# Interleaving the leftover tokens, storing the last block over 128 partitions, and six-bank bursts, in a fused linear-attention and MLP kernel

## The chip, the cores and the metric

The kernel runs on one core of one Trainium2 chip. The metric is the device time of one execution in microseconds (us), the median of several executions; lower is better. Five engines work side by side on instruction streams of their own and meet only at semaphores: PE multiplies matrices, DVE and ACT work on vectors, POOL does the same[...], and SP issues transfers. PSUM has eight banks of 128 partitions by 512 numbers of 32 bits; in this program every matmul result lives in one bank or a half of one until DVE or ACT has read it.

## What is computed

The reference, cut to what matters:

```python
scale = 1 / sqrt(sqrt(64))
def phi(x):                                  # x: (8 batches, 8 heads, 576 tokens, 64)
    h = x @ omega.T - sum(x * x) / 2         # 128 features
    return exp(h - max(h)) / sqrt(128)
q_p, k_p = phi(q * scale), phi(k * scale)
kv  = einsum('bhsm,bhsd->bhmd', k_p, v);  z = k_p.sum(axis=2)
x   = (q_p @ kv) / (q_p @ z + 1e-6)          # attention, 4608 tokens x 512
h   = x @ w_in                               # 512 -> 2048
g   = h * clip(h + 3, 0, 6) / 6
out = g @ w_out                              # 2048 -> 512, float32
```

Each batch has 576 tokens. The kernel handles the first 512 of a batch as one block of the MLP (blocks 0 to 7). The last 64 tokens of each of the eight batches, the leftovers, are gathered in a buffer `xS` of 512 columns and are the ninth block, number 8.

## The kernel before

Every operation of the program is an object with its engine, the buffers that it reads and writes, and a function that emits it. They are numbered in the order in which the Python code makes them. A table `ORDER` lists, for each engine, those numbers in the order in which the engine is to run them. The waits follow from the buffers. So a change of the table moves work in time without changing what is computed.

**Attention scores in bursts.** From batch 3 on (`ROWS = 3`), the feature projections of keys and queries run as bursts. The contraction is only 64 long, so two matmuls run side by side in the upper and the lower half of the PE array. Between bursts PE works with the whole array.

```python
BURSTS = [[(0, 2)], [(2, 6)], [(6, 10)], [(10, 14)], [(14, 18)]]
...
def burst(n, ranges):
    parts = [(d0, d1, [Virt(ring, True) for _ in range(2 if d1 - d0 == 2 else 4)]) for d0, d1 in ranges]
    ...
    for part in parts:                       # e: one operation of PE
        for x in range(d1 - d0):
            for lh in range(2):
                E.matmul(...128 columns..., kT[64*lh:64*lh+64, d0+x, :], om[64*lh:64*lh+64, lh, :], ...)
        for lh in range(2):
            E.matmul(...256 or 512 columns..., om[64*lh:64*lh+64, lh, :], qT[64*lh:64*lh+64, d0:d1, :], ...)
```

A `Virt` is a PSUM bank held from the first write until the last read. A burst over two chunks holds two banks, one over four holds four. ACT reads each with `exp`.

**Leftover tokens.** After the attention of a batch its 64 leftover tokens lie in `xb`, one token to a partition. Batch 0 turns them on PE. The others turn them by a transposing transfer, straight into their 64 neighbouring columns of `xS`:

```python
op("SP", ..., lambda E: E.dma_start_transpose(
    xS[:, :, 64 * b:64 * b + 64], xb[pb][0:64, NJ * 512:XW]), ..., writes=[("xS", b)], group="dxS", ...)
```

**The MLP.** Block 0 and blocks 1 to 6 use 512-column matmuls for the first product (`mm1`); blocks 7 and 8 use a scheme with seven products in place of eight (`mm1_pair`), with sums of inputs and weights made beforehand (`x_sums`, `input_sums`). The second product uses that scheme from block 1 on (`products`), with sums of token activations made on POOL and, for the last block, also on DVE (`token_sums`, `last_sum`).

**The last block's stores.** A row of the result of block 8 is a leftover token of some batch. With batch after batch in `xS`, the 128 tokens of a quarter of the block come from two batches, so partitions 0 to 63 and 64 to 127 go to different places and each store is made twice, over 64 partitions:

```python
x = out.rearrange("(t a s) e -> a s t e", a=2, s=S)
parts = [(64 * a, 64, x[a, MAIN:S, 2 * i:2 * i + 2, c0:c1]) for a in range(2)]
```

The last product is cut in three (256, 128 and 128 columns), and each piece is added to what is there (`C12.8` on DVE) and stored, again twice:

```python
for n, (j, e0, e1) in enumerate(((0, 0, 256), (1, 0, 128), (1, 128, 256))):
    ... P8.6n on PE: 8 matmuls of e1 - e0 columns
    ... C12.8n on DVE: osb[:, j, 256+e0:256+e1] = psum + u3
    for x in range(2):
        ... E.dma_start(ends[x, MAIN:S, j, 256+e0:256+e1], osb[64*x:64*x+64, j, 256+e0:256+e1])
```

That makes twelve stores for block 8, issued from SP and ACT.

Of the kernel before, what the change touches and what calls it, by code (L numbers as in the profile page):

```python
# [20 lines left out]
        118, 13, 124, 139, 144, 156, 115, 150, 168, 147, 153, 133, 127, 121, 142, 162, 165, 183, 171, 159, 175, 177,  # L21
        136, 185, 212, 130, 173, 197, 214, 179, 219, 254, 199, 187, 181, 242, 227, 189, 204, 202, 257, 229, 244, 217,
        222, 403, 404, 232, 234, 415, 247, 416, 417, 409, 410, 249, 411, 405, 406, 412, 418, 207, 421, 424, 252, 237,
        260, 280, 427, 430, 433, 300, 436, 288, 284, 282, 439, 286, 442, 306, 303, 445, 290, 315, 324, 309, 448, 451,
        312, 292, 294, 454, 296, 318, 457, 298, 333, 321, 583, 584, 331, 573, 337, 574, 335, 575, 339, 585, 586, 587,
        327, 341, 588, 576, 353, 345, 589, 343, 577, 329, 355, 366, 578, 579, 593, 368, 379, 371, 594, 595, 358, 392,
        590, 384, 381, 394, 397, 580, 374, 596, 597, 598, 361, 387, 603, 400, 599, 600, 621, 627, 624, 639, 636, 604,
        630, 642, 645, 505, 651, 492, 660, 501, 654, 495, 657, 486, 605, 507, 511, 606, 503, 607, 474, 509, 666, 483,
        498, 477, 480, 672, 608, 669, 513, 489, 609, 792, 610, 675, 519, 782, 515, 517, 527, 783, 539, 798, 541, 544,
        532, 551, 785, 529, 786, 563, 793, 556, 565, 568, 553, 695, 795, 796, 702, 799, 801, 802, 723, 805, 806, 709,  # L30
        736, 809, 815, 716, 824, 812, 818, 830, 741, 827, 839, 833, 842, 748, 854, 848, 845, 750, 860, 738, 760, 857,
        772, 753, 863, 765, 970, 774, 777, 971, 762, 980, 973, 974, 981, 883, 986, 983, 984, 890, 987, 989, 990, 897,
        1003, 1000, 1012, 997, 993, 994, 1006, 911, 1015, 924, 1021, 1027, 929, 1018, 936, 1033, 1030, 904, 926, 1048,
        1042, 1036, 941, 938, 1045, 960, 1051, 1174, 1158, 1159, 965, 948, 962, 1168, 953, 950, 1161, 1071, 1169,
        1162, 1078, 1171, 1172, 1175, 1085, 1177, 1178, 1191, 1092, 1185, 1188, 1194, 1200, 1215, 1203, 1112, 1206,
        1209, 1218, 1181, 1182, 1124, 1117, 1224, 1221, 1230, 1236, 1114, 1099, 1239, 1233, 1126, 1136, 1346, 1347,
        1129, 1141, 1138, 1356, 1148, 1349, 1150, 1153, 1350, 1357, 1259, 1287, 1359, 1360, 1266, 1362, 1365, 1366,
        1273, 1363, 1379, 1376, 1373, 1382, 1388, 1300, 1394, 1369, 1302, 1312, 1391, 1305, 1314, 1397, 1370, 1317,
        1406, 1336, 1409, 1418, 1338, 1403, 1421, 1412, 1280, 1424, 1427, 1550, 1341, 1534, 1535, 1544, 1454, 1537,
        1545, 1447, 1324, 1538, 1326, 1329, 1547, 1548, 1461, 1551, 1553, 1468, 1557, 1554, 1488, 1475, 1490, 1558,  # L40
        1500, 1493, 1561, 1502, 1505, 1512, 1579, 1517, 1514, 1567, 1582, 1524, 1570, 1526, 1600, 1529, 1591, 1564,
        1615, 1609, 1594, 1576, 1606, 1585, 1612, 1660, 1673, 1597, 1663, 1629, 1665, 1676, 1702, 1630, 1668, 1678,
        1689, 1632, 1633, 1692, 1639, 1694, 1705, 1681, 1718, 1707, 1640, 1697, 1731, 1721, 1642, 1723, 1643, 1734,
        1710, 1747, 1736, 1648, 1649, 1760, 1726, 1750, 1739, 1807, 1645, 1763, 1752, 1646, 1765, 1820, 1755, 1810,
        1652, 1812, 1653, 1836, 1768, 1823, 1776, 1825, 1815, 1777, 1839, 1849, 1828, 1841, 1779, 1852, 1865, 1844,
        1854, 1780, 1878, 1868, 1786, 1857, 1870, 1881, 1787, 1894, 1883, 1792, 1907, 1873, 1886, 1897, 1789, 1899,
        1793, 1790, 1910, 1902, 1939, 1912, 1795, 1796, 1915, 1799, 1800, 1923, 1924, 1933, 1934, 1926, 1927, 1936,
        1937, 1940, 1943, 1944, 1960, 1952, 1956,
    ],
    "SP": [  # L50
        0, 21, 17, 32, 23, 22, 31, 19, 25, 26, 27, 24, 29, 28, 30, 269, 270, 271, 469, 473, 472, 471, 470, 592, 602,
        468, 688, 467, 582, 693, 402, 692, 691, 694, 612, 689, 547, 535, 690, 559, 571, 572, 880, 879, 881, 804, 876,
        756, 744, 808, 768, 780, 882, 877, 781, 878, 992, 1067, 996, 1069, 1068, 1070, 932, 1065, 944, 968, 956, 969,
        1066, 1064, 1255, 1184, 1257, 1256, 1258, 1180, 1120, 1252, 1253, 1144, 1132, 1156, 1157, 1254, 1440, 1443,
        1445, 1446, 1368, 1372, 1444, 1441, 1320, 1442, 1344, 1308, 1332, 1345, 1496, 1520, 1508, 1532, 1556, 1560,
        1533, 1651, 1655, 1798, 1802, 1950, 1948, 1949, 1947, 1962, 1959,
    ],
    "ACT": [
        18, 20, 138, 119, 140, 145, 141, 157, 148, 154, 169, 151, 134, 166, 143, 211, 163, 184, 135, 172, 160, 196,
        176, 178, 241, 174, 186, 213, 225, 226, 180, 243, 182, 203, 190, 218, 188, 233, 407, 413, 419, 422, 425, 281,  # L60
        238, 261, 431, 253, 434, 428, 301, 289, 285, 437, 440, 287, 307, 443, 304, 446, 310, 449, 316, 452, 313, 455,
        325, 319, 297, 299, 295, 352, 334, 322, 336, 340, 332, 458, 342, 328, 338, 354, 378, 377, 330, 367, 344, 380,
        346, 393, 375, 362, 388, 401, 622, 591, 628, 625, 640, 631, 581, 601, 637, 643, 652, 646, 493, 661, 506, 655,
        496, 658, 502, 508, 512, 487, 504, 475, 478, 481, 673, 484, 499, 490, 667, 510, 526, 514, 611, 676, 538, 670,
        516, 520, 528, 518, 540, 550, 784, 561, 562, 787, 564, 696, 698, 700, 708, 705, 707, 703, 731, 726, 729, 701,
        724, 735, 728, 715, 714, 710, 737, 712, 816, 717, 810, 719, 813, 721, 819, 746, 828, 759, 831, 825, 840, 843,
        834, 770, 846, 722, 849, 761, 771, 855, 773, 861, 864, 858, 972, 888, 886, 884, 891, 893, 889, 896, 895, 900,
        975, 1004, 1001, 902, 898, 903, 920, 923, 998, 1013, 1007, 914, 912, 916, 1016, 1022, 1019, 1028, 917, 1034,
        1031, 907, 905, 910, 909, 1043, 1037, 946, 1049, 1052, 947, 1046, 1160, 949, 1076, 1072, 1074, 1163, 1084,
        1083, 1081, 1079, 1077, 1086, 1090, 1088, 1091, 1093, 1192, 1095, 1111, 1186, 1098, 1189, 1201, 1204, 1195,  # L70
        1134, 1123, 1207, 1216, 1210, 1125, 1097, 1225, 1219, 1222, 1231, 1237, 1102, 1100, 1105, 1137, 1234, 1240,
# [331 lines left out]
def _emit(nc, es, q, k, v, omega, w_in, w_out, out):  # L403
# [38 lines left out]
    def sbt(name, shape, dt):  # L442
        return es.enter_context(nc.sbuf_tensor(name, list(shape), dt))
# [1049 lines left out]
```

The softmax here doesn't subtract the row's maximum and nothing guards it: scores larger than these inputs give would overflow.

## Time and profile before

| what | value |
|---|---|
| device time, three runs | 309.53 us median (307.55, 309.53, 787.75) |
| the profiled run | 308.06 us on the device, 306.2 us from first to last instruction |
| PE clock granted | 0.998 of full |
| busy: PE, DVE, ACT, POOL | 97%, 80%, 69%, 76% of the span |
| chain that ended last | 79% PE, 10% POOL, 4% transfers |
| transfers | 44.88 MB in 90147 packets, mean 147 GB/s |

In the profile, an "L" with a number is a line of the kernel's source: L766 and L769 are the two kinds of matmul of a burst, L1047 is the first product of blocks 1 to 6, L1126 that of blocks 7 and 8, L1305 the second product, L1371 the last product, L1379 the last addition, L1383 and L1400 stores, L594 and L621 loads, L1233 the sums. "PE" counts matmuls and "PEld" the loading of the fixed operand, which overlaps. The ends of matmuls are modelled, so a matmul of 512 columns shows 379 ns though the next begins earlier: intervals between starts are to be used, not the durations. "SPq" and "ACTq" are the issuing of transfers on those engines.

### The profile page before, as it was taken

How to read it: one execution, taken by the hardware profiler on the slowest of the kernel's cores; microseconds unless marked ns; L12 is line 12 of the kernel's file. 1: busy time of each engine (PE TensorE's matmuls, PEld its weight loads, DVE VectorE, ACT ScalarE, POOL GpSimd, SP SyncE). 2: the span in 40 equal slices, each digit the busy share in tenths (PEclk: the TensorE clock that was granted, in tenths of full speed). 3: DMA queues.
4: the chain of work that ended last, by engine and by line, in shares of the span. 5: the costliest groups of instructions: out<-in, count | busy, mean ns of one | idle time of the engine just before them, and what ended most of it. 6: DMA issues, size and time to landing. Idle time of an engine off the chain costs nothing.

```text
span 306.2 us, 7368 instructions
## 1 busy us (share of the span) xinstructions
PE 297.7 (97%) x2798; PEld 210.4 (69%) x2798; DVE 245.7 (80%) x539; ACT 212.8 (69%) x511; POOL 233.7 (76%) x247
## 2 busy tenths in 40 slices
PE   7999999999999999999999999999999999999993
PEld 5668866545785468646856586647764788888883
DVE  3978887779898885798596877896889898999953
ACT  4995997578959972889477758876875876675300
POOL 2775657089894989799989896988845999999950
PEclk9999999999999999999999999999999999999999
DMA  8999999999972999999949984998906000210125
GB/s 224 297 187 187 269 163 153 209 206 181 194 187 35 165 143 182 242 155 208 175 104 124 217 222 112 131 130 215 207 20 190 9 0 3 94 45 3 69 88 120
DMA packets 90147, 44.88 MB, mean 147 GB/s; under 512 B 57984, under 2 KB 87808, under 8 KB 90112
## 3 DMA queue, kind: packets, MB, share of 16 engines
q1 hardware_dynamic: 62368, 30.98, 43.5%
q0 software_dynamic: 26592, 12.46, 34.1%
q10 hardware_dynamic: 1152, 0.98, 1.2%
q8 instruction: 22, 0.36, 0.5%
q14 instruction: 13, 0.11, 0.2%
HBM read 36.73 MB, written 9.44 MB: 151 GB/s over the span
## 4 chain that ended last, share of the span: by engine, by line
PE 79%; POOL 10%; DMA 4%; DVE 2%; issue 1%; SPq 1%; ACT 1%; POOLq 0%
PE p L1305 28%; PE p L1047 25%; PE p L1126 5%; PE p L1217 4%; POOL gT L1233 3%; PE p L1192 3%; PE p L978 3%; DMA wi<-in_moe_w_in_dram 3%; POOL s L1233 3%; PE p L950 2%; PE p L766 2%; PE p L769 2%; DMA q<-in_q_dram 1%; SPq L621 1%; PE p L830 1%
## 5 line engine op out<-in xcount | busy, mean ns | idle before, releaser
L1047 PE MATMUL p<-xT,wi 128*128 128x512 f16 x384 | 90.3, 379 | 0.0
L1055 DVE SCALAR_TENSOR_TENSOR gT<-tsb,p 128x512 f16<-128x512 f16 x96 | 62.8, 679 | 12.4 <-ACT tsb L1053 11.6
L1053 ACT ACTIVATE tsb<-p 128x512 f16<-128x512 f32 x96 | 55.4, 600 | 16.5 <-PE p L1047 12.3
L1047 PEld LDWEIGHTS p<-xT,wi 128*128 128x128 f16 x384 | 35.4, 98 | 38.0 <-issue 1.1
L1305 PE MATMUL p<-wo,gT 128*128 128x256 f16 x368 | 45.8, 273 | 0.1
L1233 POOL TENSOR_TENSOR s<-gT 128x512 f16<-128x512 f16 x30 | 34.8, 1161 | 6.8 <-DVE gT L1055 4.8
L1233 POOL TENSOR_TENSOR gT<-gT,s 128x512 f16<-128x512 f16 x31 | 35.8, 1155 | 5.2 <-PE p L1305 3.0
L1233 POOL TENSOR_TENSOR s<-gT,s 128x512 f16<-128x512 f16 x31 | 35.8, 1156 | 4.9 <-DVE gT L1055 2.9
L1305 PEld LDWEIGHTS p<-wo,gT 128*128 128x128 f16 x368 | 35.0, 98 | 6.1 <-issue 0.8
L1233 POOL TENSOR_TENSOR gT<-gT 128x512 f16<-128x512 f16 x31 | 36.1, 1164 | 2.4
L934 POOL TENSOR_TENSOR vc<-v,cc 128x512 bf16<-128x512 f32 x24 | 25.4, 1057 | 12.3 <-DVE cc L928 7.4
L790 DVE TENSOR_REDUCE mx<-kp 128x4 f32<-128x512 bf16 (+1 forms) x50 | 29.9, 619 | 5.0 <-ACT kp L785 5.0
L794 ACT ACTIVATE qpT<-p 128x512 bf16<-128x512 f32 (+1 forms) x50 | 26.9, 564 | 8.6 <-PE p L769 8.6
L785 ACT ACTIVATE kp<-p 128x512 bf16<-128x512 f32 (+1 forms) x50 | 26.2, 559 | 9.3 <-PE p L769 8.6
L1305 PE MATMUL p<-t,gT 128*128 128x256 f16 x256 | 31.4, 273 | 0.0
L994 DVE TENSOR_TENSOR xb<-p,rec 128x256 f16<-128x256 f32 (+1 forms) x64 | 28.8, 471 | 0.6
L621 POOL DMA_DIRECT2D qb<-in_q_dram x28 | 19.5, 705 | 11.5 <-PE p L1047 9.6
L1305 PEld LDWEIGHTS p<-t,gT 128*128 128x128 f16 x256 | 24.3, 98 | 5.1 <-issue 1.2
L522 ACT COPY p<-p 128x256 f32<-128x256 f32 (+1 forms) x46 | 17.7, 398 | 13.2 <-PE p L1126 5.6
L1174 ACT ACTIVATE tsb<-p 128x512 f16<-128x512 f32 x32 | 18.8, 598 | 6.5 <-PE p L1126 3.9
L621 POOL DMA_DIRECT2D kb<-in_k_dram x21 | 16.5, 786 | 7.1 <-PE p L1047 7.1
L1176 DVE SCALAR_TENSOR_TENSOR gT<-tsb,p 128x512 f16<-128x512 f16 x32 | 21.0, 679 | 0.9 <-ACT tsb L1174 0.8
(132 smaller groups left out, 580.4 us busy)
## 6 DMA issues: line engine op xcount, KB each, us to landing
v<-in_v_dram SPq DMA_DIRECT2D x14, 512.0 KB, 4.9
out_dram<-osb SPq DMA_DIRECT2D x14, 512.0 KB, 3.3
kb<-in_k_dram POOLq DMA_DIRECT2D x14, 256.0 KB, 5.4
qb<-in_q_dram POOLq DMA_DIRECT2D x14, 256.0 KB, 5.6
wo<-in_moe_w_out_dram POOLq DMA_DIRECT2D x8, 256.0 KB, 8.2
wi<-in_moe_w_in_dram POOLq DMA_DIRECT2D x3, 512.0 KB, 7.4
q<-in_q_dram SPq DMA_DIRECT2D x4, 256.0 KB, 4.5
vl<-in_v_dram SPq DMA_DIRECT2D x8, 128.0 KB, 4.1
```

What stands on the lines that cost most here:

```text
L621: lambda E: E.dma_start(dst, src), prio + 0.001 * turn_of[0], reads=gate, writes=keys,
L785: op("ACT", actt(128 * (d1 - d0)), lambda E, lh=lh, ko=ko, part=part: E.activation(ko, out_of(part, 0, lh)[0].rearrange("p (x m) -> p x m" ...
L790: op("DVE", dvet(128 * (d1 - d0)), lambda E, ko=ko, mo=mo: E.reduce_max(mo, ko, axis=AX.X), p0 + 0.01, reads=[("kp", 0, d, lh) for d in ra ...
L794: op("ACT", actt(128 * (d1 - d0)), lambda E, lh=lh, part=part: E.activation(qd[:, part[0]:part[1], lh, :], out_of(part, 1, lh)[0].rearrang ...
L934: return E.tensor_tensor(vcm[:, :, 0:D], v32[:, m, :, :], cbc, ALU.mult)
L994: op("DVE", dvet(128 * n), lambda E: E.tensor_tensor(xv(i0, i1), psum()[:, :, :, 0:64], rbc, ALU.mult), t + 0.01, reads=[vn, ("rec", ru)], ...
L1047: ins = E.matmul(ring.t[vh.slot], wi[:, c, 128 * f:128 * f + 128], xv[:, c, :], start=(c == 0), stop=(c == NJ - 1))
L1053: op("ACT", actt(512), lambda E: E.activation(tsb[tu][:], ring.t[vh.slot], AF.Relu, bias=0.5, scale=1.0 / 6.0), t - 0.1, reads=[vh], write ...
L1055: op("DVE", dvet(512), lambda E: E.scalar_tensor_tensor(gT[gu][:, f, :], tsb[tu][:], 1.0, ring.t[vh.slot], ALU.min, ALU.mult), t - 0.1, re ...
L1176: op("DVE", dvet(512), lambda E, v=v, tu=tu, dst=dst: E.scalar_tensor_tensor(dst(), pieces(tsb[tu][:]), 1.0, pieces(v.ring.t[v.slot]), ALU ...
L1233: op(engines, {"POOL": 0.07 + n / 455.0, "DVE": 0.1 + n / 850.0}, lambda E: E.tensor_tensor(dst, x, y, ALU.subtract if minus else ALU.add) ...
L1305: ins = E.matmul(ring.t[v.slot][:, 256 * j:256 * j + 256], a[:, f, 128 * j:128 * j + 128], w[:, f, :], start=(first and f == 0 and j == 0) ...
```

## The change

It has four parts.

1. The leftovers are interleaved: column 256·(b // 4) + 4·s + b % 4 of `xS` holds leftover token s of batch b. A transposing transfer[...] writes a small buffer `xs0`, and a copy on ACT or POOL puts it into `xS`. Batch 0 writes the pattern from PSUM directly.
2. With that, the 128 tokens of a quarter of block 8 are 32 tokens of four batches, which one pattern in memory can address. Each store of the last block goes once over 128 partitions: nine in place of twelve.
3. The first two bursts of a batch (two and four banks) become one of six banks.
4. A new table `ORDER` for all engines.

The diff without the table:

```diff
-    BURSTS = [[(0, 2)], [(2, 6)], [(6, 10)], [(10, 14)], [(14, 18)]]
+    BURSTS = [[(0, 2), (2, 6)], [(6, 10)], [(10, 14)], [(14, 18)]]
...
+    xs0 = [sbt("xs0_%d" % u, [128, NJ, 64], F16) for u in range(2)]
...
-            op(EV_T, both(256), evac(lambda: xS[:, :, 64 * b:64 * b + 64],
+            op(EV_T, both(256), evac(lambda: woven(b),
...
             op("SP", 0.6, lambda E: E.dma_start_transpose(
-                xS[:, :, 64 * b:64 * b + 64], xb[pb][0:64, NJ * 512:XW]),
-               pos(12), ..., writes=[("xS", b)], group="dxS", inc=16, lat=1.0,
+                xs0[pb][:], xb[pb][0:64, NJ * 512:XW]),
+               pos(12), ..., writes=[("xs0", pb)], group="dxS%d" % pb, inc=16, lat=1.0,
                name="Sdma.%d" % b, issue=1.2, packet=24.0)
+            op(("ACT", "POOL"), {"ACT": 0.4, "POOL": 0.6}, evac(lambda: woven(b), lambda: xs0[pb][:]), pos(12) + 0.05,
+               reads=[("xs0", pb)], writes=[("xS", b)], name="Swv.%d" % b)
+
+    def woven(b):
+        c = 256 * (b // 4) + b % 4
+        return xS[:, :, c:c + 253:4]
...
+    def leftovers(r):
+        s0 = MAIN + 32 * (r % 2)
+        return out.rearrange("(i b s) e -> i s b e", b=4, s=S)[r // 2, s0:s0 + 32]
...
-            for x in range(2):
-                op(("SP", "ACT"), ..., E.dma_start(
-                    ends[x, MAIN:S, j, 256 + e0:256 + e1], osb[64 * x:64 * x + 64, j, 256 + e0:256 + e1]), ...)
+            op(("SP", "ACT"), ..., E.dma_start(
+                leftovers(j)[:, :, 256 + e0:256 + e1], osb[:, j, 256 + e0:256 + e1]), ...)
...
-            x = out.rearrange("(t a s) e -> a s t e", a=2, s=S)
-            parts = [(64 * a, 64, x[a, MAIN:S, 2 * i:2 * i + 2, c0:c1]) for a in range(2)]
+            parts = [(r, 1, leftovers(r)[:, :, c0:c1]) for r in (2 * i, 2 * i + 1)]
```

The part of the table that orders the end, with the numbers turned into the operations that they stand for (`outw` and `outl` are stores of block 8, `outl` those of the last product's pieces):

| engine | before | after |
|---|---|---|
| PE | P8.3 P8.4 P8.5 P8.62 P8.60 P8.61 | P8.3 P8.4 P8.62 P8.61 P8.5 P8.60 |
| DVE | C22.8 u4.8 C21.8 C12.82 C12.80 C12.81 | C22.8 u4.8 C12.81 C12.82 C21.8 C12.80 |
| SP | outw ×4, outl2, outl1 | outw ×2, outl1, outl2, outw, outl0 |
| ACT | outw ×2, outl0, outl2, outl0, outl1 | outw ×3 |

At the start, SP's first eight loads of batch 0 were keys (left), keys, queries (left), queries, queries, queries (left), keys, queries. They become keys (left), keys, queries, keys, queries, queries, queries, queries (left): the 256 KB pieces of queries come earlier, the 64 KB pieces of leftover queries later. The first loads of `w_in` on POOL wait for one of those 256 KB pieces; it was the eighth load on SP and is now the sixth. On the vector engines some operations change places: of the copies into `xS`, those of batches 1, 2 and 5 are on ACT and those of 3, 4, 6 and 7 on POOL; of the sums near the end, three go from DVE to POOL and two from POOL to DVE.

## The prediction

> **What bounds the kernel now.** I read the table of stretches first. Columns: the stretch in us, its length, then the busy time of PE, PE's operand loads, DVE, ACT and POOL with instruction counts in brackets, the granted clock, the share of the transfer engines, GB/s.
>
> ```profile
> 20.00:30.00 10.00, 9.48 (x109) 7.79 (x109) 8.26 (x25) 6.42 (x16) 4.62 (x7) 1.00 1.39 185
> 30.00:100.00 70.00, 69.93 (x639) 45.88 (x637) 57.93 (x123) 57.35 (x137) 47.00 (x55) 1.00 0.96 177
> 100.00:228.00 128.00, 127.76 (x1241) 84.14 (x1240) 100.28 (x227) 94.36 (x234) 110.83 (x115) 1.00 0.98 164
> 228.00:290.00 62.00, 61.72 (x529) 50.02 (x528) 58.05 (x111) 39.54 (x89) 53.59 (x46) 1.00 0.15 49
> 301.40:306.20 4.80, 0.00 (x0) 0.00 (x0) 0.30 (x2) 0.00 (x0) 0.00 (x0) 0.84 0.66 145
> ```
>
> From 30 to 290 us PE is idle for 0.07 + 0.24 + 0.28 = 0.6 us in 260. Because matmul ends are modelled, "busy" alone proves little, so I check the rate on the chain of waits:
>
> ```profile
> 158.14 5.29 PE p L1047 x24
> 288.01 11.61 PE p L1305 x104
> ```
>
> The first is 220 ns for each 512-column matmul, the second 112 ns for each of 256. At the 2.4 GHz that the Trainium skill gives ("TensorE: Matmul & The Clock Gate", the part on the measured gap, which states columns over 2.4 GHz plus about 2.5 ns) these would be 216 and 109. The trace agrees within 3%. PE really streams. Counting by the groups by shape: 472 matmuls of 512 columns x 0.220 = 104 us; 1363 of 256 x 0.1105 (between the 0.109 of an undisturbed run and the 0.112 above) = 151; 576 of 65 columns, which in the timeline follow each other by some 31 ns, = 18; some 120 of 128 x 0.056 = 7; 32 of 130 x 0.06 = 2; the bursts, below, 15. The sum is 297 us, against a last matmul that ends at 301.4. So in the middle there are waits of a few tenths, in the first 30 us of about 3 (PE idle 2.04 before 10 us, then 0.53 and 0.52), and after the last matmul 4.8 us in which PE has nothing. 63 of the 256-column matmuls (7 us) are fillers that keep PE busy while it waits for the first data. The change can gain at the two ends and at the bursts; it removes no matmul.
>
> **The Trainium skill** on the parts concerned. "SBUF — State Buffer", section "Door 1", says that partitions 0 to 63 reach only 8 of 16 ports, so a 64-partition transfer has half the rate; "DMA: Bandwidth & Descriptors", section on the anatomy of one transfer, puts a fixed cost of about 2 us on each. The list of transfer issues agrees with the second and shows why the first matters little here:
>
> ```profile
> out_dram<-osb SPq DMA_DIRECT2D x4, 128.0 KB, 2.5
> out_dram<-osb ACTq DMA_DIRECT2D x2, 32.0 KB, 2.5
> ```
>
> A fourfold size doesn't change the 2.5 us to landing. "TensorEngine Tiling (Array Packing)", "Gotcha 1: PSUM Pressure", says that row tiles write different banks: a burst therefore asks for its banks all at once.
>
> **Part 1, the stores at the end.** The timeline of the last 5 us (start, length, engine, line, operation, count):
>
> ```profile
> 300.99 0.74 DVE L1379 TENSOR_TENSOR osb<-p,u 128x256 f32<-128x256 f32 x2 [0.43 <-PE p L1371]
> 301.04 1.26 SPq L1400 DMA_DIRECT2D out_dram<-osb  x2
> 301.12 0.27 PE L1371 MATMUL p<-wo,gT 128*128 128x128 f16 x2
> 301.44 2.60 ACTq L1383 DMA_DIRECT2D out_dram<-osb  x4
> 302.35 1.24 SPq L1383 DMA_DIRECT2D out_dram<-osb  x2
> ```
>
> The last addition ends at 300.99 + 0.74 = 301.73. Nothing is computed after that, yet ACT issues four stores until 304.04 (2.60 / 4 = 0.65 us each). The last of these starts about 303.4, lands some 2.2 us later, and the program closes 0.5 us after. From the last addition to the end: 306.2 − 301.73 = 4.45 us, of which some 1.7 us is the queue of issues. Afterwards the last product's pieces need three issues in place of six, and by the new order the pieces of 128 columns and their stores are done before the last matmuls. After the last addition (`C12.80`) only one store remains, and one on the same queue a little ahead of it (`outw`, released by `C21.8` about 0.4 us earlier, 0.62 us to issue). So: 0.2 us wait for the queue + 2.5 us to landing + 0.5 us close = 3.2 us, 1.25 less. Against that, the last piece on PE is now 256 wide, so its addition takes 0.42 and not 0.29 us, and `C21.8` (0.69 us) runs just before it: PE's end to DVE's end grows from 0.34 to about 0.6 us. **Net −1.0 us**, all on the path.
>
> **Part 2, six-bank bursts.** A burst alone, and two bursts that already lie side by side in the kernel before:
>
> ```profile
> 150.03 1.04 PE L1305 MATMUL p<-wo,gT 128*128 128x256 f16 x8
> 150.99 0.40 PE L766 MATMUL p<-om,kT 64*128 64x128 bf16 x8
> 151.23 0.38 PE L769 MATMUL p<-qT,om 64*128 64x512 bf16 x2
> 151.54 0.94 PE L1305 MATMUL p<-wo,s 128*128 128x256 f16 x7
> ...
> 180.73 0.60 PE L1305 MATMUL p<-t,s 128*128 128x256 f16 x4
> 181.26 0.29 PE L766 MATMUL p<-om,kT 64*128 64x128 bf16 x4
> 182.12 0.61 PE L1305 MATMUL p<-wo,s 128*128 128x256 f16 x4
> ```
>
> Eight matmuls from 150.03 at 0.109 reach 150.90; the burst starts at 150.99: 0.09 lost on entry. It streams four pairs of 128 columns and one of 512, 1024 columns or 0.427 us, to 151.42; the next starts at 151.54: 0.12 lost on exit. So 0.21 us a burst. For the two together: 181.17 to 181.26 on entry, 0.640 us of columns to 181.90, next at 182.12: 0.31 us, where two alone lose 0.42. A merge saves 0.11 us. There are five, one of them side by side before already: 4 x 0.11 = **−0.4 us**. It is on PE's path, if ACT empties six banks in time: four `exp` of 256 and four of 512 columns, at 0.39 and 0.60 us about 3.5 us with their overlaps, in which PE must live on the two other banks. The new order puts each of these bursts beside pieces of the second product, which hold a bank for a long time, and I count no loss for it.
>
> **Part 3, the interleaving.** Seven more copies of 128x256. On ACT a copy of that size (`xT` in the groups) is 0.37 us: 3 x 0.37 = 1.1 us at 69% busy, hidden. On POOL the only conversion, 128x512, is 0.61 us; I take 0.45 for half of it with a stride, an estimate: 4 x 0.45 = 1.8 us. Two of them precede the sums of the last block, where POOL is the nearly full engine: 53.59 of 62 us from 228 to 290, and nothing but sums at one per 1.23 us from 243 on. The moves of sums between the engines add one more (three in, two out) for POOL: 1.23 us. Late sums reach PE: before the pieces that start at 249.71 and 288.01 the chain of waits runs through POOL for several us, yet PE waited only 0.31 and 0.30 us there (from the starts of its matmuls). The new order regroups just these sums (`P8.2` comes first, the last `S4` goes to DVE). I count **+0.4 us**.
>
> **Part 4, the start.** The chain of waits in the first 30 us runs through the loads:
>
> ```profile
> 5.47 4.40 DMA q<-in_q_dram
> 19.88 8.67 DMA wi<-in_moe_w_in_dram
> 28.69 1.91 PE p L1192 x16
> ```
>
> `w_in` waits for that q piece, landed at 9.87 us, the eighth load of SP; it becomes the sixth, and two pieces of 64 KB are no longer ahead of it. Loads land about 0.6 us apart there, so the gate opens about 1 us earlier. But POOL now does a cast (0.61) and a copy between the pieces of `w_in`, and the last piece is still behind two key loads with the transfer engines full (share over 1). Of the 1 us I count half: **−0.5 us**.
>
> **The sum**: −1.0 − 0.4 + 0.4 − 0.5 = −1.5 us on a span of 306.2, so 304.7. The profiled run took 308.06 on the device, 1.9 above its span: 306.6. The three runs scatter by 2 us without the disturbed one, so a median may lie a little higher; I say **306.8**.
>
> **Rivals.** (a) POOL becomes the bound of the last two blocks. For it: 1.23 + 0.9 us more work in a solid stretch, and PE waits there for POOL already. Against it: DVE takes other sums and the order was made for it. It would give 306.8 + 1.3 = 308. (b) A six-bank burst finds the banks taken and PE waits for ACT: five times, at most some 0.6 us each, +3 us, or 309.5; for it speaks that ACT's reads of bursts already make the groups `kp` and `qpT` wait on PE in clumps, against it that before, two bursts side by side passed with 0.31 us. (c) The start gains all that is idle there, 3 us in place of 0.5: 304.3. Against it, the transfers share is over 1 from 10 us on. (d) The end gains nothing because landing dominates: 307.8; against it, the issues visibly queue for 1.7 us.
>
> **Range and chances.** (a), (b) and (d) bound the upper side, (c) the lower: 304.6 to 309.3. Faster by over 2% would need 303.3, beyond (c); slower by over 2% needs 315.7, six us of new waits in a PE stream that has 0.6. So 0.05 faster, 0.92 within 2%, 0.03 slower.
>
> **What would show it.** Right: from the last addition to the end about 3.2 us in place of 4.45, one store issued after it; 20 entries into bursts in place of 24, each merged one losing about 0.3; `w_in`'s first issue near 9.1 us; PE idle from 30 to 290 us no more than 1 us. Wrong: PE waiting for POOL sums by more than 1 us after 228; gaps before bursts above 0.2 us, ended by ACT; the last `w_in` piece landing later than 28.5 us.

## The result, and the profile after

The changed kernel takes **303.57 us** (median of five, 303.2 to 304.12) against 308.15 us before: a ratio of 0.985, 95% interval 0.982 to 0.988. Measured once more in a later set of runs beside the kernel before, it took 303.74 us at a ratio of 0.980 (0.976 to 0.985). So it is 1.5 to 2% faster. The prediction of 306.8 us and its range (304.6 to 309.3) both lie above that. The span of the profiled run fell from 306.2 to 301.8 us, by 4.4; 1.5 was predicted.

The table of stretches after, with the columns explained in the prediction (stretch, length, busy time of PE, its operand loads, DVE, ACT and POOL, clock, transfers):

```profile
20.00:30.00 10.00, 10.00 (x123) 8.88 (x122) 9.45 (x27) 8.23 (x20) 4.54 (x8) 1.00 1.37 185
30.00:100.00 70.00, 69.65 (x634) 45.65 (x632) 57.50 (x125) 57.29 (x141) 48.54 (x58) 1.00 1.09 177
100.00:224.00 124.00, 123.89 (x1178) 81.70 (x1176) 98.81 (x222) 91.72 (x227) 106.26 (x111) 1.00 0.96 168
224.00:286.00 62.00, 62.00 (x574) 50.79 (x573) 58.17 (x118) 40.96 (x94) 57.07 (x52) 1.00 0.15 45
```

From 20 to 30 us PE is no longer idle at all (0.52 us before). In the 62 us from 224 us POOL is busier than before in the like stretch (57.07 against 53.59 us), and PE is idle for 0.00. The rate of matmuls hasn't changed; on the chain of waits after:

```profile
66.62 4.32 PE p L1054 x20
```

4.32 / 20 = 216 ns for a 512-column matmul. The end, in the timeline (start, length, engine, line, operation, count, and in brackets what ended the idle time):

```profile
297.51 1.04 PE L1381 MATMUL p<-wo,gT 128*128 128x256 f16 x8
297.71 0.69 DVE L1328 TENSOR_TENSOR osb<-p 128x512 f32<-128x512 f32 x1 [0.56 <-PE p L1312]
298.43 0.54 SPq L1408 DMA_DIRECT2D out_dram<-osb  x1
298.58 0.42 DVE L1389 TENSOR_TENSOR osb<-p,u 128x256 f32<-128x256 f32 x1 [0.18 <-PE p L1381]
299.04 0.58 SPq L1392 DMA_DIRECT2D out_dram<-osb  x1
```

The last addition ends at 299.01 (298.58 + 0.42, rounded), one store is issued after it, and the program ends at 301.77: 2.76 us later, where it was 4.45.

**Where the 4.4 us are.** Busy time can't say, because matmul ends are modelled. So I took the intervals between the starts of all 2800 matmuls and subtracted from each the streaming time (columns over 2.4 GHz plus 2.5 ns, as in the prediction; in rows of equal matmuls the starts are 216 ns apart for 512 columns and 109 for 256). What remains was sorted by kind: the time of fillers, gaps over 30 ns (waits), gaps at the entry and exit of bursts, and small gaps.

| part | before | after | difference | predicted |
|---|---|---|---|---|
| fillers and waits before 45 us | 12.44 | 11.33 | −1.11 | −0.5 |
| waits from 45 us on | 1.42 | 0.79 | −0.63 | +0.4 |
| entries and exits of bursts | 4.64 (24) | 3.88 (20) | −0.76 | −0.4 |
| start of the last matmul to the end | 4.99 | 3.49 | −1.50 | −1.0 |
| gaps under 30 ns, rest | | | −0.4 | 0 |
| sum | | | −4.4 | −1.5 |

Every term came out better than predicted, so no single step explains the miss. The experiments take the terms one at a time. Two limits hold for all of them: the runs scatter (the kernel after from 303.2 to 305.6 us, the kernel before in one set from 307.5 to 312.5), in part with the landing of the first loads, and each profile is one run. So differences below 1 us are read in the trace, at the place concerned, and a median is used where it is larger. The kernel before drifts from one set of runs to the next (medians 308.2 to 310.8 us); ratios compare with the kernel before in the same set, and their 95% intervals stand in brackets.

### The profile page after: what moved, and what is told of

It reads as the page before. It is cut to its first block, busy times and chain, and to the rows that moved or that the text cites. A ratio compares the mean times of both kernels' runs of the same rounds, so it can differ in the third digit from the quotient of the medians.

```text
span 301.8 us, 7410 instructions
## 1 busy us (share of the span) xinstructions
PE 295.8 (98%) x2800; PEld 211.4 (70%) x2800; DVE 246.8 (82%) x547; ACT 214.5 (71%) x516; POOL 237.0 (79%) x255
## 4 chain that ended last, share of the span: by engine, by line
PE 91%; ACT 5%; DVE 2%; issue 0%; ACTq 0%
PE p L1312 32%; PE p L1054 25%; PE p L1133 8%; PE p L1199 5%; PE p L1224 5%; PE p L985 3%; PE p L957 3%; PE p L767 2%; PE p L770 2%; PE p L811 1%; PE p L831 1%; PE p L576 1%; ACT vc L943 1%; DVE mx L822 1%; ACT tsb L1060 1%; PE p L535 1%
## 5 line engine op out<-in xcount | busy, mean ns | idle before, releaser
L1240 POOL TENSOR_TENSOR gT<-gT 128x512 f16<-128x512 f16 x32 | 37.0, 1155 | 3.2 <-DVE gT L1062 1.0
L1240 POOL TENSOR_TENSOR s<-gT 128x512 f16<-128x512 f16 x31 | 36.2, 1167 | 3.8 <-DVE gT L1062 1.7
L1240 POOL TENSOR_TENSOR gT<-gT,s 128x512 f16<-128x512 f16 x30 | 34.7, 1157 | 2.4
L795 ACT ACTIVATE qpT<-p 128x512 bf16<-128x512 f32 (+1 forms) x50 | 27.6, 572 | 7.7 <-PE p L770 7.1
L941 POOL TENSOR_TENSOR vc<-v,cc 128x512 bf16<-128x512 f32 x22 | 23.4, 1064 | 9.5 <-DMA v<-in_v_dram 3.3
L523 ACT COPY p<-p 128x256 f32<-128x256 f32 (+1 forms) x42 | 16.4, 403 | 14.9 <-PE p L1312 8.6
L943 ACT ACTIVATE vc<-v,cc 128x64 bf16<-128x64 f32 x80 | 20.3, 348 | 0.0
```

The lines of the kernel that those rows point to most:

```text
L795: op("ACT", actt(128 * (d1 - d0)), lambda E, lh=lh, part=part: E.activation(qd[:, part[0]:part[1], lh, :], out_of(part, 1, lh)[0].rearrang ...
L941: return E.tensor_tensor(vcm[:, :, 0:D], v32[:, m, :, :], cbc, ALU.mult)
L943: ins = E.activation(vcm[:, i, 0:D], v32[:, m, i, :], AF.Copy, scale=cc[pb][:, c0 + i:c0 + i + 1])
L1240: op(engines, {"POOL": 0.07 + n / 455.0, "DVE": 0.1 + n / 850.0}, lambda E: E.tensor_tensor(dst, x, y, ALU.subtract if minus else ALU.add) ...
```

## The experiments

### The end: nine stores, or their order

**oldend**: nine stores, old order of the last pieces.

```diff
 PE:  P8.3 P8.4
-     P8.62 P8.61 P8.5 P8.60
+     P8.5 P8.62 P8.60 P8.61
 DVE: C22.8 u4.8
-     C12.81 C12.82 C21.8 C12.80
+     C21.8 C12.82 C12.80 C12.81
 SP:  outw outw
-     outl1 outl2 outw outl0          ACT: outw outw outw
+     outw outl2 outl1                ACT: outw outw outw outl0
```

> The kernel after with its nine stores, but with the old order of the last pieces: on PE the 256-column product P8.5 ahead of the three last pieces P8.62, P8.60, P8.61, on DVE C21.8, C12.82, C12.80, C12.81. Theory B (the order gives the gain of the end): four stores are released within 1.4 us and queue on two engines, so last addition to end is about 3.3 us in place of 2.76, less 0.3 for the narrower last piece: 303.8 to 304.2 us. Rival A (the number of stores gives it): 303.3 to 303.7 us, equal to the kernel after or a little shorter because the last piece has 128 columns.

**twelve**: the new order, but no interleaving, no copies, twelve stores.

```diff
-    c = 256 * (b // 4) + b % 4;  xS[:, :, c:c + 253:4]
+    xS[:, :, 64 * b:64 * b + 64]
-    leftovers(j)[:, :, 256 + e0:256 + e1]        # one store, 128 partitions
+    for x in range(2): ends[x, MAIN:S, j, ...]   # two stores, 64 partitions each
```

> The kernel after without the interleaving: batch after batch in xS, no copies from xs0, and twelve stores of 64 partitions for the last block; merged bursts and the new order of the end are kept. Theory A (the smaller number of stores gives the end its gain): the second store of the last addition queues for 0.6 us on one of the two issuing engines, so last addition to end grows from 2.76 to 3.4 to 3.9 us and the time to 304.2 to 304.8 us. Rival B (the order gives it, stores overlap on two issuing engines): 2.8 to 3.0 us from last addition to end, 303.4 to 303.8 us, or less, since seven copies of some 0.77 us on ACT and POOL are gone.

**oldend12**: both edits together.

> The kernel after with both halves of the new end undone: batch after batch in xS without copies, twelve stores, and the old order of the last pieces and of their stores; merged bursts, start and middle as in the kernel after. From the start of the last matmul to the end of the span: 4.99 us before, 3.49 after, 3.91 with twelve stores in the new order, 3.07 with nine in the old order. If stores and order act together: 4.8 to 5.0 us, so 304.9 to 305.3 us. If something else in the new order of the whole shortened the end: 3.9 us or less, 304.0 us.

| | time, us | ratio to before | last matmul to end | waits of PE after 280 us |
|---|---|---|---|---|
| twelve stores, old order (oldend12) | 306.3 | 0.989 (0.985–0.992) | 4.89 | 0.43 |
| twelve stores, new order (twelve) | 305.0 | 0.986 (0.983–0.989) | 3.91 | 0.31 |
| nine stores, old order (oldend) | 304.65 | 0.985 (0.982–0.988) | 3.07 | 0.30 |
| nine stores, new order (after) | 303.57, 303.74 | 0.985, 0.980 | 3.49 | 0.00 |

In the timeline of oldend12 the queue of the kernel before is back, six issues behind the additions:

```profile
298.56 0.74 DVE L1384 TENSOR_TENSOR osb<-p,u 128x256 f32<-128x256 f32 x2 [0.43 <-PE p L1376]
299.01 2.59 ACTq L1388 DMA_DIRECT2D out_dram<-osb  x4
299.92 1.24 SPq L1388 DMA_DIRECT2D out_dram<-osb  x2
```

and with nine stores in the same old order the last three are issued as fast as they are released:

```profile
298.31 1.32 SPq L1397 DMA_DIRECT2D out_dram<-osb  x2
298.32 0.74 DVE L1394 TENSOR_TENSOR osb<-p,u 128x256 f32<-128x256 f32 x2 [0.43 <-PE p L1386]
298.78 0.55 ACTq L1397 DMA_DIRECT2D out_dram<-osb  x1
```

In the traces either edit shortens the end: the stores alone by 4.89 − 3.07 = 1.8 us, the order alone by 1.0 us. They remove the same queue, so together they don't add up to 2.8 but give 1.4. With nine stores the tail is even shorter in the old order (its last piece is 128 wide), but there PE waits 0.30 us ahead of P8.5 for DVE to free a bank, so the two orders come to 3.37 and 3.49 us. The profiled run of oldend (303.39 us) was the fastest of its six; why its median is 1 us above that of the kernel after is not settled.

**best1, best3**: one 128-column piece ahead of P8.5 to cover that wait, the short pieces last; best3 also swaps the engines that issue the last two stores.

```diff
-PE:  P8.62 P8.61 P8.5 P8.60      DVE: C12.81 C12.82 C21.8 C12.80
+PE:  P8.62 P8.5 P8.60 P8.61      DVE: C12.82 C21.8 C12.80 C12.81
-best1:  SP outl1, ACT outl0
+best3:  SP outl0, ACT outl1
```

> The kernel after with another order of the last pieces: on PE P8.62, P8.5, P8.60, P8.61, on DVE C12.82, C21.8, C12.80, C12.81, so that one 128-column piece covers the wait for DVE that the old order showed before P8.5 (0.30 us) and the last addition is a short one. If both hold: 3.07 us from the start of the last matmul to the end as with the old order, without its wait, so 0.4 us less than the kernel after, 303.2 us. If the wait comes back or the stores queue: 303.6 us.

> The kernel after with the last pieces in the order P8.62, P8.5, P8.60, P8.61, as tried once, but with the 256-column store on SP and the last 128-column store on ACT. In the first try ACT took 0.86 us to issue the 256-column store and that one landed last. If the issue alone was to blame: 3.1 to 3.3 us from the start of the last matmul to the end, 0.2 to 0.4 us less than the kernel after. If an issue from ACT is always late here: 3.4 us or more, no gain.

best1 took 303.97 us (ratio 0.981, 0.978–0.984), best3 303.59 (0.980, 0.975–0.984) beside 303.74 for the kernel after in the same set. The wait before P8.5 disappeared in both. In best1 ACT needed 0.86 us for the 256-column store, which landed last: 3.46 us from the last matmul to the end. In best3 it is 3.21 us, 0.3 less than after, as expected. That is a tenth of a per cent, and no time shows it. From here the landing (some 2 us after the last issue) and the close are what is left.

### The bursts: banks, or entering and leaving the half-array form

The merged burst at 151 us in the timeline of PE alone, after:

```profile
151.41 0.29 PE L767 MATMUL p<-om,kT 64*128 64x128 bf16 x4
151.54 0.27 PE L770 MATMUL p<-qT,om 64*128 64x256 bf16 x2
151.65 0.39 PE L767 MATMUL p<-om,kT 64*128 64x128 bf16 x8
151.87 0.38 PE L770 MATMUL p<-qT,om 64*128 64x512 bf16 x2
152.18 0.50 PE L1312 MATMUL p<-t,gT 128*128 128x256 f16 x3
```

From 151.41 to 152.18 are 0.77 us, of which 0.64 stream: 0.13 on exit; with 0.10 on entry, 0.22 for a burst of six banks. A burst of four loses 0.10 + 0.12, the same, and one of two in the kernel before 0.10 + 0.11. So it is a cost for each entry, whatever the size.

One of the five merged bursts loses 0.31 us, as the two side by side in the kernel before did, from which the prediction took its size. There the array's form is not all. In the kernel before, with DVE and the operand loads of PE:

```profile
181.37 0.69 DVE L1321 TENSOR_TENSOR u<-p 128x512 f32<-128x512 f32 x1 [0.58 <-PE p L1305]
...
182.12 0.55 PEld L1305 LDWEIGHTS p<-wo,s 128*128 128x128 f16 x6 [0.35 <-DVE u L1321]
```

The product that follows the burst starts when DVE has read a bank (181.37 + 0.69 = 182.06). At the merged burst of 117.57 us, after, its next product waits for the same operation of DVE. So about 0.09 of the 0.31 us is a wait for a bank.

**split**: the burst cut in two, one operation of PE between the parts. **adjacent**: cut in two, nothing between.

```diff
-    BURSTS = [[(0, 2), (2, 6)], [(6, 10)], [(10, 14)], [(14, 18)]]
+    BURSTS = [[(0, 2)], [(2, 6)], [(6, 10)], [(10, 14)], [(14, 18)]]
 PE, for each batch b from 3 on:
-    R b.0               <next operation>
+split:     R b.0  <next operation>  R b.1
+adjacent:  R b.0  R b.1  <next operation>
```

> The kernel after, but with the first burst of each of the five batches cut again into one of two banks and one of four, with one operation of PE in full-array form between them. Theory A (each entry into and exit from the half-array form costs about 0.21 us on PE): five more entries and exits, 0.8 to 1.0 us longer than the kernel after, so about 304.5 us against 303.6. Rival B (what the bursts save is only turned into waits elsewhere, or six banks at once cost waits): no longer than the kernel after, 303.3 to 303.8. In the profile, A expects 25 entries in place of 20 and waits of PE elsewhere unchanged.

> The kernel after with the merged burst cut again into one of two banks and one of four, but side by side, with nothing between them. The array stays in its half form from one to the other. Theory E (the cost is entering and leaving the half form): the same 20 entries, so no more than 0.1 us for each of the five, 304.0 us against 303.6 at most, and spans within 0.5 us. Rival W (the cost of the cut is that the second burst waits for its own four banks): waits of 0.3 to 0.7 us at three of the five, 1 us or more longer, as when one operation lay between.

split took **307.08 us** (0.995, 0.993–0.997), 3.4 above the kernel after; adjacent took **303.70** (0.980, 0.976–0.983), as much as the kernel after. In adjacent the pair of 154.19 us streams as one burst (timeline of PE alone):

```profile
154.19 0.28 PE L772 MATMUL p<-om,kT 64*128 64x128 bf16 x4
154.31 0.27 PE L775 MATMUL p<-qT,om 64*128 64x256 bf16 x2
154.42 0.39 PE L772 MATMUL p<-om,kT 64*128 64x128 bf16 x8
154.65 0.38 PE L775 MATMUL p<-qT,om 64*128 64x512 bf16 x2
154.96 0.50 PE L1317 MATMUL p<-t,gT 128*128 128x256 f16 x3
```

0.77 us again. So the merge as such gives nothing; what counts is that the array stays in its half form. "TensorEngine Tiling (Array Packing)" of the Trainium skill says in its section "Key Properties" that changing the tiling mode drains the engine. The traces agree and give the price: about 0.10 us in, 0.12 out.

In split the five further entries cost 5 x 0.22 = 1.1 us, and a second cost came that theory A did not have. It falls not on the second part but on the next burst after it. In batch 4 the parts start at 119.75 and 121.59 us, neither late, and the next burst is due at about 124.0. Its timeline, with ACT, DVE, PE and PE's operand loads:

```profile
123.95 1.19 ACT L791 ACTIVATE kp<-p 128x512 bf16<-128x512 f32 x3
124.09 0.69 DVE L1333 TENSOR_TENSOR osb<-p,u 128x512 f32<-128x512 f32 x1 [0.18 <-PE p L1317]
...
124.64 0.22 PEld L772 LDWEIGHTS p<-om,kT 64*128 64x128 bf16 x8 [0.86 <-ACT kp L791]
124.64 0.40 PE L772 MATMUL p<-om,kT 64*128 64x128 bf16 x8 [0.58 <-ACT kp L791]
```

It starts when ACT has read banks for `kp`. In three of the five batches the next burst was late by 0.2 to 0.65 us beyond the entry, each time with ACT ending the wait, and after one first part PE waited 0.53 us for DVE. Why these three, and how the operation between the parts brings it about, is not shown. In all, the bursts lose 2.7 us more than in the kernel after, and waits from 45 us on 0.5 us more (new ones at 206.78 and 209.46 us): 3.2 of the 3.4 us. The profiled run, 308.43 us, was the slowest of 16 and lost 1.6 us more at its start, where `w_in` landed late.

### The start

**loads_old**: only SP's first loads in the old order. **front_old2**: all engines' operations of the first batch in the old order. **front_new**: the kernel before with all engines' operations of the first batch in the new order.

```diff
 loads_old, SP:
-k-left k q k q q q q-left ...
+k-left k q-left q q q-left k q ...
 front_old2, front_new: the table's entries for the first batch, on all engines, from the other kernel
```

> The kernel after with the old order of SP's first loads alone; all other engines as in the kernel after. Theory G (the gate: w_in waits for the sixth load in place of the eighth): w_in's first issue goes from 9.49 us to about 10.2, its last piece lands 0.5 to 1.5 us later, PE waits for it, 304.3 to 305.5 us. Rival E (the order of the other engines did it): within 0.3 us of the kernel after.

> The kernel after with the order of the kernel before for the first batch's operations on all engines. Theory S (the new start gives 1.1 us, as fillers and waits in the first 45 us say: 12.44 us before, 11.33 after): fillers and waits near 12.4 us in the first 45 us and 304.5 to 305 us. Rival N (the start is worth nothing, another part gave its share): 303.4 to 304.0 us.

> The kernel before with the order of the kernel after for the operations of the first batch only: its loads, the loads and casts of w_in, the attention of batch 0 and its first product. Nothing else is changed. Theory S (the new order of the start gives about 1 us: w_in's last piece lands at 26.95 in place of 28.55 us and the waits between 20 and 30 us, 1.28 us, disappear): 306.9 to 307.4 us against 308.15. Rival N (fillers and other waits take its place): 307.9 to 308.3 us.

loads_old took 305.45 us (0.986, 0.981–0.991), 1.7 to 1.9 above the kernel after. Fillers and waits in the first 45 us of its trace are 12.58 us against 11.33, so to undo SP's order alone in the kernel after costs 1.25 us. But not through `w_in`: its first issue moved to 10.48 us and its last piece landed at 28.25, and PE did not wait for it. The time was gone earlier:

```profile
12.20 0.61 POOL L529 CAST qb<-q 128x512 bf16<-128x512 f32 x1 [0.77 <-DMA q<-in_q_dram]
...
12.86 0.67 PEld L540 LDWEIGHTS p<-ident,qb 128*128 128x128 bf16 x12 [0.39 <-POOL qb L529]
12.86 0.84 PE L540 MATMUL p<-ident,qb 128*128 128x128 bf16 x12
```

A query piece lands late, POOL waits for it, PE waits for POOL's cast; around such waits stand 1.2 us more fillers (8.30 against 7.10). Their number is set when the program is built, from its own estimate of the start times: 76 here, 65 after, 63 before.

This is not what the order of the loads gained over the kernel before. Up to 20 us that kernel loses 11.1 us in fillers and waits, the kernel after 11.3, loads_old 12.2: the loads and the order of the other engines fit each other, and this mixture is worse than both. The 1.1 us between the two kernels lie between 20 and 33 us. About 0.6 are small waits from 20 to 22.5 us, where the attention of batch 0 meets the first product: 0.7 us in all five profiles with the old order of the first batch, 0.1 after. The other 0.6 are PE's wait for the last piece of `w_in`, here in the kernel before, with POOL's issue of that piece before and after:

```profile
28.69 1.03 PE L1192 MATMUL p<-xT,wi 128*128 128x256 f16 x8 [0.44 <-DMA wi<-in_moe_w_in_dram]
...
19.88 0.76 POOL L594 DMA_DIRECT2D wi<-in_moe_w_in_dram  x1
...
20.09 0.76 POOL L595 DMA_DIRECT2D wi<-in_moe_w_in_dram  x1
```

After, it is issued 0.2 us later than before, and landed earlier (26.95 against 28.55 us) because the transfer took 6.87 us in place of 8.67. That is within its scatter, below.

front_old2 took 306.29 us (0.988, 0.983–0.992): 12.26 us of fillers and waits in the first 30 us, 0.9 more than after, and another 1.55 between 30 and 45 us, at the seam where the old order meets the new. front_new took 308.33 against 309.02 us (0.996, 0.994–0.998), 0.5 to 1.9 us less; in its profiled run SP's second load landed at 7.20 us in place of 5.8 to 6.6 in the others (but for adjacent, 7.83), so that trace is not used for sizes.

**after_again**, **before_again**: the two kernels unchanged. **wi_early**: the last `w_in` piece ahead of two key pieces on POOL's queue; **best4**: the same with best3's end.

```diff
 POOL:
-vcc.0.3  kl.1  k00.1  wi3  k10.1
+vcc.0.3  wi3  kl.1  k00.1  k10.1
```

> The kernel after once more, unchanged, beside the two kernels of this call. If the differences of the single parts are real and not drift between calls, it takes 303.4 to 304.0 us, and its profile shows the same waits after 45 us as before (0.79 us, at 86.75 and 204.76).

> The kernel before, profiled a second time, to see which of its waits come back. If the waits after 45 us (1.42 us) are set by the order they come back within 0.2 us; those of the start depend on when loads land and may differ by 1 us.

> The kernel after with the last piece of w_in issued ahead of two key pieces of the next batch on POOL's queue, about 1.5 us earlier. Theory J (the landing of this piece, 26.95 us in one run and 29.33 in another, against a need at about 28 us, makes the scatter of the kernel after): it lands near 25.5 to 27.5 us, no run over 304.5 us, median 303.2 to 303.6. Rival K (key pieces of the next batch come late instead): PE waits for keys between 30 and 40 us, 304 us or more.

> The earlier w_in piece together with the last pieces in the order P8.62, P8.5, P8.60, P8.61 and the last store on ACT. If both hold: 303.0 to 303.4 us. If the earlier piece only moves the wait: 303.8 us or more.

In the profile of after_again (a run of 305.61 us, the slowest of six; the others took 303.19 to 304.24) PE shows the wait that the kernel after didn't have:

```profile
29.46 0.60 PE L1199 MATMUL p<-xT,wi 128*128 128x256 f16 x4 [1.37 <-DMA wi<-in_moe_w_in_dram]
```

Here `w_in`'s last piece landed at 29.33 us. Over the runs with the new start it lands between 26.95 and 27.9, or, four times, between 29.1 and 30.2; with the old order of all first operations between 27.5 and 28.7, once at 30.2. PE needs it at about 28. So the new start leaves some slack in most runs and none in the rest. wi_early brought the landing to 24.90 us and best4 to 25.68. But now keys were late, by 0.33 and 0.67 us (waits at 25.39 and 26.17 us), as rival K had it, though earlier than it said, and the times are 304.36 us (0.983, 0.979–0.988) and 304.02 (0.981, 0.977–0.985): nothing gained. Of the waits of the kernel before after 45 us, those at 70, 193, 250 and 288 us came back in before_again (309.94 us) with the same length, and one of 0.24 us was new; they belong to the order.

### The interleaving and the sums

**nine_before2**: the kernel before with interleaving, copies and nine stores, and its own order everywhere.

```diff
 the kernel before, and
+    xs0, woven(b), leftovers(r)                 # as in the change
+    ACT:  Swv.1 Swv.2 Swv.5
+    POOL: Swv.3 Swv.4 ... X2.7 ... Swv.6 Swv.7 X1.8
```

In a first form of this table, nine_before, POOL had a sum of block 8 ahead of the copy of batch 7 that it reads. In that order the engines end up waiting for each other, so it has no time.

> The kernel before with its own order everywhere (start, bursts, sums, last pieces), but with the interleaving, its seven copies (three on ACT, four on POOL, two of them ahead of the sums of the last block), and nine stores of 128 partitions. Theory E (the copies cost PE nothing and the end gains by the number of stores alone): 4.99 us from the start of the last matmul to the end fall to about 3.1 us, no wait of PE grows, ratio to the kernel before 0.993 to 0.995. Theory P (as the prediction had it, copies on POOL delay the sums of the last blocks): PE waits for POOL grow by 0.4 us or more after 193 us, ratio 0.996 or above.

It took **310.88 us** against 309.54, a ratio of 1.003 (1.001–1.006), although its end is 1.9 us shorter (3.05 us from the last matmul). The medians overstate the loss: twelve of its 22 runs had a granted clock of 0.993 or 0.994 and a median of 311.5 us, the other ten 0.999 or 1.0 and 309.3, and the kernel before, with 25 of 27 runs at 0.996 or more, took 309.3 in these. So gain and loss about cancel, as in the spans of the profiled runs (306.5 against 306.2 us). The chain that delays it, in POOL's timeline and then PE's:

```profile
242.70 1.57 POOL L528 COPY xS<-xs 128x256 f16<-128x256 f16 x2
244.36 1.16 POOL L1244 TENSOR_TENSOR q<-xS 128x512 f16<-128x512 f16 x1
245.59 1.16 POOL L1244 TENSOR_TENSOR s<-gT,s 128x512 f16<-128x512 f16 x1
...
251.97 1.05 PE L1316 MATMUL p<-t,s 128*128 128x256 f16 x8 [1.98 <-POOL s L1244]
```

In the kernel before the like wait is 0.31 us, the first of three for POOL late in the program (PE's operand loads and PE):

```profile
249.71 0.55 PEld L1305 LDWEIGHTS p<-t,s 128*128 128x128 f16 x6 [0.42 <-POOL s L1233]
288.01 0.44 PEld L1305 LDWEIGHTS p<-wo,gT 128*128 128x128 f16 x5 [0.41 <-POOL gT L1233]
...
193.37 0.43 PE L950 MATMUL p<-vc,kp 128*128 128x65 bf16 x8 [0.22 <-POOL vc L934]
```

In nine_before2 POOL runs without a gap from 234 us to that sum. The two copies sit in the middle of the row, 1.66 us with the spacing between operations, and the wait of PE grows from 0.31 to 2.14 us. So the mechanism of the prediction's part 3 is real, and larger than it said: on the old order the interleaving takes 1.8 us there and gives back 1.9 at the end. In the new order the loss does not appear. In the kernel after the last two copies on POOL start at 231.2 and 247.6 us and PE waits for neither; and `twelve`, which has no copies at all, shows the same two waits between 45 and 280 us as the kernel after (0.51 us at 87, 0.21 at 205; after, 0.51 and 0.25). There the copies cost PE no wait that the trace shows.

Their own duration was underestimated by about half. The operations that write `xS`, in the view of that buffer, after, and the one that turns batch 0's leftovers from PSUM, before:

```profile
L524 POOL COPY xS<-xs x4: 758/759/764, 148.5 to 247.6; 128x256 f16<-128x256 f16 x4
L523 ACT COPY xS<-xs x3: 760/780/811, 91.7 to 217.4; 128x256 f16<-128x256 f16 x3
...
L523 ACT CAST xS<-p x1: 757/757/757, 33.5 to 33.5; 128x256 f16<-128x256 f32 x1
```

```profile
L522 ACT CAST xS<-p x1: 405/405/405, 28.0 to 28.0; 128x256 f16<-128x256 f32 x1
```

The columns are line, engine, operation, count, then least, median and greatest duration in ns, the first and last start in us, and the forms. The last line of the first fence and the line of the second are the same operation with an output step of 8 bytes and of 2: 757 against 405 ns.

**sums_old**: three sums of block 8 back on their old engines. **back_new**: the kernel before with the new order of blocks 7 and 8 and of the second product of block 6.

```diff
 sums_old:
-POOL: ... S38.2 ... S18.3 S48.0 S48.1          DVE: ... S48.3 S48.2
+POOL: ... S48.0 S48.1 S48.2                    DVE: ... S38.2 ... S18.3 ... S48.3
```

> The kernel after with three sums of block 8 on the engines of the kernel before: S38.2 and S18.3 on DVE, S48.2 on POOL; interleaving copies and all else stay. POOL has one sum of 1.15 us less in all, but its last one, S48.2, comes after two others. Theory O (it counts where a sum lies in the order, not how full POOL is): PE waits 0.3 to 1 us near the end of block 8, 304.0 to 304.5 us. Rival P (POOL's load is what counts): no wait of PE, time as the kernel after or up to 0.2 us less.

> The kernel before (contiguous leftovers, separate bursts, old start, old order of the last pieces, twelve stores) with the order of the kernel after only for blocks 7 and 8 and the second product of block 6: their sums, which engine makes each sum, and the matmuls that read them. Theory O (the order, not the interleaving, took away the waits of PE for sums): the waits after 220 us, 0.69 us in the kernel before, fall below 0.15 and the time by about 0.6 us, so a ratio of 0.998 to the kernel before. Rival P (POOL is the limit there, as the prediction had it, or new waits arise where old and new order meet): 0.3 us or more of waits stay, ratio 1.000 or above.

sums_old took 304.73 us (0.982, 0.978–0.986). POOL has one sum less, and yet PE waits for it:

```profile
295.72 0.45 PE L1386 MATMUL p<-wo,gT 128*128 128x128 f16 x5 [0.32 <-POOL gT L1245]
```

This wait of 0.32 us on POOL (0.48 between the starts of PE's matmuls) isn't in the kernel after. Here the place of a sum in the order counted, and not the sum of POOL's work. The rest of the difference to 303.6 us is in the start of that run. back_new took 311.94 us (1.008, 1.006–1.011) and decides nothing: new waits of 1.27 and 0.77 us arose at 133 and 145 us, where the moved operations meet the old ones, and more after 240 us. This part of the table could not be moved alone.

## Why the prediction was wrong

It had the right four places and the right direction for three, and summed to a third of the gain. The largest miss is part 3, 1.0 of the 2.9 us.

- **Part 1, the stores.** Right in mechanism: one store after the last addition, the issues no longer queue. The sum "0.2 us wait for the queue + 2.5 us to landing + 0.5 us close = 3.2 us" was too large: there was no wait for the queue, and landing took 2.24 us after the issue began (299.04 to 301.28). Measured 2.76 us in all, and −1.5 in place of −1.0 on the path. Rival (d) fell.
- **Part 2, the bursts.** The wrong term is "A merge saves 0.11 us". It came from the one pair of side-by-side bursts in the kernel before, with 0.31 us lost, and took all of that for entry and exit, though the product behind the pair was waiting for DVE. In adjacent four pairs of five lose 0.22 and only one 0.31. A merge saves a whole entry and exit, 0.21 us, and four of them give the 0.76 measured. Rival (b), ACT and six banks, did not happen in the kernel after; waits for ACT came in split, at the bursts behind the cut ones.
- **Part 3, the interleaving.** The step "+0.4 us" failed, in sign. The estimate of 0.45 us for a copy on POOL was too small (0.76), and the danger was real: 1.8 us on the old order. What failed was to charge this cost to the new order, in which PE waits for no copy. The prediction saw that the order regroups the sums, and the waits for POOL in the kernel before (0.38, 0.31 and 0.30 us) were in its view; it counted them as a sign of POOL's fullness and not as something that a new order can remove. After 45 us the waits fell by 0.63 us: those three and one of 0.24 us at 70 us went, one of 0.51 us at 87 us (for DVE) and one of 0.25 at 205 came. They belong to the kernels and not to chance (before_again, after_again), and neither to the interleaving nor to the merge, since neither twelve nor adjacent shows one of the four. That leaves the new order; which of its moves did it is not shown.
- **Part 4, the start.** "The gate opens about 1 us earlier" was 0.7 us (10.18 to 9.49 us), and none of it reached the last piece of `w_in`, issued 0.2 us later than before: with more work ahead of the last piece POOL had lost all of it by then. So "of the 1 us I count half" failed as a path, and part of the 1.1 us that came is luck. The 0.6 us of the wait for `w_in` went because one transfer took 6.87 us in place of 8.67, and in after_again that wait was back, 1.5 us long. The small waits from 20 to 22.5 us, 0.6 us less, were not in the sum at all.
- **The range.** Its lower side was rival (c) alone. Each of the four terms was sized from its cautious side (a queue that stays, the costlier pair, half of the opening gate, a cost for POOL), so the errors had one sign; a range built from one rival at a time could not hold that.

What stays open: which moves of the table removed the waits after 45 us (sums_old shows one move that brings a new wait) and the small waits from 20 us on, and the 0.4 us of gaps under 30 ns and rest.

## What to carry to other kernels

Where many small transfers end a program, count the issues that fall behind the last result; fewer stores and an earlier order remove the same queue, so don't add their gains. Where a nearly full engine feeds the critical one, ask where in its row a new operation lies: 1.6 us of copies cost PE 1.8 us in one order and no wait in the other. When a wait is used to size a cost, look at what ended it: 0.09 us of waiting for DVE, counted as a cost of the array's form, halved the gain of a merge. A new order of a tuned program can collect the waits that the old trace shows, so list these one by one and ask of each whether something speaks against its removal.

## What the runs showed of the hardware

- Each entry into the half-array form with the exit from it costs PE about 0.22 us together, for bursts of two, four or six banks alike; where it was 0.31 (one six-bank burst in five), the next product waited for DVE.
- A copy with an output step of 8 bytes took 757 ns on ACT where the one with a step of 2 bytes took 405. "SBUF — State Buffer" of the Trainium skill, in the note on cachelines under "Door 1", puts 16-byte lines with at least two hits each at full bandwidth, and 8 numbers of 16 bits as a step that is free. A step of 4 such numbers nearly doubled the time here; the measurement decides.
- The same load of 512 KB (`w_in`'s last piece) took from 6.9 to 9.0 us to land over the profiled runs of kernels that have the same instructions up to there.
- In several traces (split, twelve, oldend) a few gaps of 214 to 222 ns stand in rows of matmuls with no releaser, as long as one matmul of 512 columns and as many as there are records too few (five, 2795 of 2800, in each of the three). They are taken as missing records and left out of the sums above.
